# Attention with two window masks and a slot mixture on one core: constants built on chip, longer DRAM runs for phi and w1, output halves evacuated by two engines

## The chip, the cores and the metric

The kernel runs on one core of one Trainium2 chip. Its engines have instruction queues of their own and meet only at semaphores: TensorE (PE in the profile, its weight loads PEld), VectorE (DVE), ScalarE (ACT), GpSimd (POOL) and SyncE (SP). Transfers between DRAM and the on-chip memory (SBUF) are issued from an engine's queue and carried out by 16 DMA engines. Matmuls write to PSUM[...]. The metric is the time of one execution on the device in microseconds (us), median of several runs.

## The reference

Eight batches of eight-head attention over 576 positions with head dimension 64, followed by a soft mixture of experts over all 4608 rows.

```python
scores = scale * np.matmul(q, k.transpose(0, 1, 3, 2))
rel = pos[:, None] - pos[None, :]
mask_plain = (rel >= 0) & (rel < window)                                   # heads 0 to 3, window 32
mask_dil = (rel >= 0) & (rel < window * dilation) & (rel % dilation == 0)   # heads 4 to 7, dilation 4
...                                          # softmax over keys, times v, heads side by side: x, 4608 x 512
logits = x @ phi                             # 4608 x 32 slots
d = softmax(logits, over rows);  slot_input = d.T @ x          # 32 x 512
h = np.maximum(slot_input[e] @ w1[e], 0.0);  slot_out[e] = h @ w2[e]   # four slots for each of 8 experts
c = softmax(logits, over slots);  return c @ slot_out          # 4608 x 512
```

Inputs and output are fp32. q, k and v hold 9.4 MB each, w1 and w2 16.8 MB each, the output 9.4 MB.

## The kernel before

All loads are cast to fp16 on the way, and all of them but two go through one queue, POOL's. Two small constants (masks and ident) come through SP's. The order on every engine is the order of the program text: the main part stands in a manual schedule.

**Prologue.** prologue() issues the loads of batch 0 in halves (q and k of the plain heads, then of the dilated heads, line 163), the constants, v of batch 0 (lines 172 and 175), phi, and then batch 1. The constants come from DRAM as fp16 arrays made ahead of time: masks (128 x 336, additive masks with -60000 where a score is masked, and in its last 32 columns a 0/1 mask for emask), ident (the 128 x 128 identity) and orders (four 128 x 128 selection matrices, repeated in each 32-row group, that put four interleaved rows of v back in order by matmul).

**Attention, per batch b, in three slots.** slot0 holds the first score group of batch b, the dilated part of batch b-1 and the sums over rows of batch b-2; slot1 the second score group and v; slot2 the third group and the logits of batch b-1. DVE transposes raw q and k into place (qk_plain, line 241; qk_dil, line 250). emit_scores() writes the mask into two PSUM tiles of two banks each, sa and sb (line 276, ident times masks), adds q times k on top (line 287) and lets ACT take the exponent (line 298). order_v_plain() uses the same two PSUM tiles to reorder v (line 188). emit_av() multiplies by v, emit_norm() divides by the row sums into xp and xd, the normalised rows x of the plain and the dilated heads. back_logits() needs x transposed (back_xT_plain, back_xT_dil) and phi4, which is phi repeated four times; back_u() accumulates d.T @ x over the batches with x as the stationary operand (line 455), in two chunks c of 128 features for each half of the heads.

**Weights.** weights() spreads the loads of w1 over the batches (load_w1, line 220: 16 loads of two 128-row chunks of one expert) and puts w2 at the end (load_w2, line 224). The w2 of experts 6 and 7 are loaded by halves of their columns (line 232). w2 is read in 8 KB runs, since each partition takes four consecutive rows.

**Queue order on POOL.** load_qk(b+2) waits until the raw buffers (two of each) are free, load_v(b+2) until v's staging has been spread, which involves two POOL copies (lines 212 and 216) that wait for DVE (line 209). Since POOL takes its instructions in order, a copy that waits also holds the loads behind it.

**Tail.** After the attention: slot inputs, hidden layer (line 645), slot outputs by column halves (line 681). Half 0 of the columns is complete before half 1; so the first 8 of 18 row pairs store their half 0 early. combine(half, pair) computes 256 rows x 256 columns: two matmuls into PSUM (line 697), scaling by the reciprocal row sum on the way to SBUF (lines 709 and 713) and a store of 256 KB issued by POOL (line 719). combine_full(pair) does both halves, with ACT on block 0 and DVE on block 1 (lines 732 and 736), and a store of 512 KB (line 743).

Of the kernel before, what the change touches and what calls it, by code (L numbers as in the profile page):

```python
# [9 lines left out]
FP32 = mybir.dt.float32  # L10
# [9 lines left out]
WINDOW = 32  # L20
# [20 lines left out]
NE = NT + DIL + 1  # L41
NFIN = N_ROWS // 128
UNITS = 7
NH = DMODEL // 2
NSPLIT = 16


def make_masks():

    a = np.arange(128)[:, None]  # L50
    rel = np.arange(WQ)[None, :] - a
    plain = (rel >= 0) & (rel < WINDOW)
    rel = 32 + np.arange(LEFT)[None, :] - a
    left = (rel >= 0) & (rel < WINDOW) & (a < 48)
    m = [plain, plain[:, 0:TAIL]] + [left] * 5
    m = [np.where(x, 0.0, -60000.0) for x in m]
    ok = ((np.arange(128)[:, None] % 32) < LEFT) & np.ones((1, N_SLOTS), bool)
    m.append(ok)
    return np.ascontiguousarray(np.concatenate(m, axis=1).astype(np.float16))


def make_orders():

    a = np.arange(128)[:, None, None] % 32
    r = np.arange(DIL)[None, :, None]
    p = np.arange(128)[None, None, :]
    return np.ascontiguousarray((p == DIL * a + r).astype(np.float16).reshape(128, DIL * 128))


@with_exitstack  # L70
def kernel(
# [9 lines left out]
):  # L81
    nc = tc.nc

    mask_np = make_masks()
    masks_dram = nc.inline_tensor(mask_np, name="masks_d")
    orders_dram = nc.inline_tensor(make_orders(), name="orders_d")
    ident_dram = nc.inline_tensor(np.eye(128, dtype=np.float16), name="ident_d")


    consts = ctx.enter_context(tc.tile_pool(name="consts", bufs=1))  # L90
    masks = consts.tile([128, mask_np.shape[1]], FP16, name="masks")
    bias = (
        masks[:, None, 0:WQ].broadcast_to([128, 3, WQ]),
        masks[:, 0 : W1 + NLEFT],
# [73 lines left out]
    def load_v(b):  # L168
        slab = fix.tile([128, V_SLAB], FP16, name=f"vs_{b}", tag=f"vs{b % 2}")
        sa, sb = (slab[:, 2048 * i : 2048 * i + 2048].rearrange("a (h n) -> a h n", h=H) for i in range(2))  # L170
        vstage[b] = (sa, sb)
        nc.gpsimd.dma_start(
            out=sa, in_=v[b, :, 0:512, :].rearrange("h (a r) d -> a h (r d)", r=DIL)
        )
        nc.gpsimd.dma_start(
            out=sb[0:LEFT], in_=v[b, :, 512:S, :].rearrange("h (a r) d -> a h (r d)", r=DIL)
        )

    def order_v_plain(b):
# [16 lines left out]
        for ab in range(2):  # L196
# [4 lines left out]
            if ab == 0:  # L201
# [2 lines left out]
                    in_=ps[0][0:TAIL, 0, 256:512].rearrange("p (h d) -> p h d", h=4),  # L204
                )

    def spread_v(b):
        sa, sb = vstage.pop(b)
        nc.vector.tensor_copy(  # L209
            out=vD[b % NV][:, :, :, 0:D], in_=sa[:, 4:8].rearrange("a h (r d) -> a h r d", r=DIL)  # L210
        )
        nc.gpsimd.tensor_copy(
            out=vL[b % NV][32 : 32 + LEFT, :, :, 0:D],
            in_=sb[0:LEFT, 4:8].rearrange("a h (r d) -> a h r d", r=DIL),
        )
        nc.gpsimd.tensor_copy(out=vL[b % NV][0:32, :, :, 0:D], in_=vD[b % NV][96:128, :, :, 0:D])  # L216

    def load_w1(e, i):
        src = moe_w1[e].rearrange("(c p) f -> p c f", p=128)
        nc.gpsimd.dma_start(out=w1t[e][:, 2 * i : 2 * i + 2, :], in_=src[:, 2 * i : 2 * i + 2, :])  # L220

    def load_w2(e, half=None):
        if half is None:
# [13 lines left out]
    def qk_plain(ti, b):  # L237
        src = raw[(ti, b)][:, 0, :].bitcast(U32).rearrange("p (j m) -> p j m", m=32)
        t = qTp[b % 2] if ti == 0 else kTp[b % 2][:, 0:S, :]
        dst = t.rearrange("p s t -> p (s t)").bitcast(U32).rearrange("p (a j) -> p j a", j=PJ)  # L240
        nc.vector.transpose(out=dst, in_=src)  # L241
# [200 lines left out]
    def back_u(b):  # L442
        up = ring.tile([128, 5, N_SLOTS], FP32, name=f"u_{b}", tag="ring")
        er = er_t.pop(b)
        jobs = []
        for t in range(NT):
            n = 128 if t < 4 else TAIL
            for c in range(2):
                jobs.append((c, xp_t[b][0:n, t, 128 * c : 128 * c + 128], er[0:n, t, :]))
            jobs.append((4, ones[0:n, :], er[0:n, t, :]))  # L450
        for r in range(DIL + 1):
            for c in range(2):
                jobs.append((2 + c, xd_t[b][:, r, 128 * c : 128 * c + 128], er[:, NT + r, :]))
        for i, (c, l, rr) in enumerate(jobs):
            nc.tensor.matmul(  # L455
                up[:, c, :], l, rr, start=(i == 0), stop=(i == len(jobs) - 1), skip_group_check=True
            )
        if b == 0:
            nc.vector.tensor_copy(out=UT, in_=up)
        else:  # L460
            nc.vector.tensor_tensor(out=UT, in0=UT, in1=up, op=ALU.add)
# [4 lines left out]
    def prologue():  # L466
        load_qk(0, 0, (0,))
        load_qk(1, 0, (0,))
        nc.sync.dma_start(out=masks, in_=masks_dram.ap())
        nc.sync.dma_start(out=ident, in_=ident_dram.ap())  # L470
        for i in range(2):
            nc.vector.memset(kTp[i][:, S : S + 64, :], 0.0)
            nc.vector.memset(kTd[i][:, S : S + 80, :], 0.0)
            nc.vector.memset(qTd[i][:, S : S + 16, :], 0.0)
            nc.vector.memset(vP[i][:, :, :, D : D + 1], 1.0)
            nc.vector.memset(vP[i][TAIL:128, 4, :, :], 0.0)
            nc.vector.memset(vD[i][:, :, :, D : D + 1], 1.0)
            nc.vector.memset(vL[i][:, :, :, D : D + 1], 1.0)
        load_qk(0, 0, (1,))
        load_qk(1, 0, (1,))  # L480
        nc.gpsimd.dma_start(out=orders.rearrange("p r n -> p (r n)"), in_=orders_dram.ap())
        load_v(0)
        nc.gpsimd.dma_start(out=phi_raw, in_=moe_phi.rearrange("(c p) s -> p c s", p=128))
        load_qk(0, 1)
        load_qk(1, 1)
        load_v(1)
        qk_plain(0, 0)
        qk_plain(1, 0)
        nc.vector.memset(ones, 1.0)
        nc.vector.memset(emask, 1.0)  # L490
        for part in range(2):
            qk_dil(0, 0, part)
        qk_dil(1, 0, 0)
# [34 lines left out]
    def slot0(b):  # L528
        att, b1, b2, b3 = b < B, b - 1 >= 0 and b <= B, 2 <= b < B + 2, b + 1 < B
        if att:  # L530
            qk_dil(1, b, 1)
            emit_scores(b, 0)
            if b + 2 < B:
                load_qk(0, b + 2)
                load_qk(1, b + 2)
            weights(b, 0)
        if b == 0:
            nc.vector.memset(ET, 0.0)
            nc.vector.memset(siTm, 0.0)
            nc.vector.tensor_copy(out=emask[:, NE - 1, :], in_=masks[:, W1 + NLEFT :])  # L540
            nc.vector.tensor_copy(
                out=phi4, in_=phi_raw[:, :, None, :].broadcast_to([128, 4, 4, N_SLOTS])
            )
        if b1:
            emit_av(b - 1, "d", 0)
            emit_norm(b - 1, "d", 0)
        if b2:
            back_erow(b - 2)
        if b1:
            emit_av(b - 1, "d", 1)  # L550
            emit_norm(b - 1, "d", 1)
            back_xT_plain(b - 1, 0)
        if att and b > 0:
            order_v_plain(b)
        if b1:
            emit_av(b - 1, "d", 2)
            emit_norm(b - 1, "d", 2)
            back_xT_plain(b - 1, 1)
        if b2:
            back_u(b - 2)  # L560
# [132 lines left out]
    def combine(half, pair):  # L693
        fp = psum_f.tile([128, 2, NH], FP32, name=f"f{half}_{pair}", tag="f")
        r0 = 256 * pair
        for k in range(2):
            nc.tensor.matmul(  # L697
                fp[:, k, :],
                ET[:, r0 + 128 * k : r0 + 128 * k + 128],
                so_sb[:, NH * half : NH * half + NH],  # L700
                start=True,
                stop=True,
                skip_group_check=True,
            )
        ot = out_pool.tile([128, 2, NH], FP16, name=f"ot{half}_{pair}", tag=f"ot{half}", bufs=NSPLIT // 2)
        if pair % 2 == 0:
            for k in range(2):
                blk = 2 * pair + k
                nc.scalar.activation(  # L709
                    out=ot[:, k, :], in_=fp[:, k, :], func=AF.Copy, scale=rrow[:, blk : blk + 1]  # L710
                )
        else:
            nc.vector.tensor_tensor(  # L713
                out=ot,
                in0=fp,
                in1=rrow[:, 2 * pair : 2 * pair + 2, None].broadcast_to([128, 2, NH]),
                op=ALU.mult,
            )
        nc.gpsimd.dma_start(  # L719
            out=out[r0 : r0 + 256, NH * half : NH * half + NH].rearrange("(k p) n -> p k n", k=2),  # L720
            in_=ot,
        )
# [74 lines left out]
```

The softmax here doesn't subtract the row's maximum and nothing guards it: scores larger than these inputs give would overflow.

## Time and profile before

Median 184.07 us of 4 runs (183.55 to 184.17).

| | |
|---|---|
| profiled execution | 184.17 us |
| its span, first to last instruction | 182.2 us |
| busy share PE, DVE, ACT, POOL | 77%, 57%, 49%, 44% |
| DMA moved, counted as landed | 41.00 MB in 32023 packets |
| read from and written to DRAM | 62.18 MB and 9.44 MB |
| median time from issue to landing, w1 (512 KB) | 16.9 us |
| the same, v (512 KB) | 13.3 us |
| the same, orders (128 KB), masks (84 KB), ident (32 KB), phi (32 KB) | 7.1, 1.8, 2.0, 8.8 us |

The page divides the span into 40 slices of 4.56 us and gives a digit of busy tenths for each. "DMA" is the mean busy share of the 16 DMA engines and can pass 1 in the tables by window, because an engine can have more than one packet under way. A group of instructions is a line of the program, engine, operation, output <- input, shapes and count, then busy time, mean ns of one, and the idle time of the engine just before them with what ended it. A time from issue to landing contains the time that a transfer waited behind others in the queue.

### The profile page before, as it was taken

How to read it: one execution, taken by the hardware profiler on the slowest of the kernel's cores; microseconds unless marked ns; L12 is line 12 of the kernel's file. 1: busy time of each engine (PE TensorE's matmuls, PEld its weight loads, DVE VectorE, ACT ScalarE, POOL GpSimd, SP SyncE). 2: the span in 40 equal slices, each digit the busy share in tenths (PEclk: the TensorE clock that was granted, in tenths of full speed). 3: DMA queues.
4: the chain of work that ended last, by engine and by line, in shares of the span. 5: the costliest groups of instructions: out<-in, count | busy, mean ns of one | idle time of the engine just before them, and what ended most of it. 6: DMA issues, size and time to landing. Idle time of an engine off the chain costs nothing.

```text
span 182.2 us, 5521 instructions
## 1 busy us (share of the span) xinstructions
PE 141.1 (77%) x2448; PEld 84.9 (47%) x2448; DVE 104.1 (57%) x225; ACT 89.8 (49%) x161; POOL 80.8 (44%) x112
## 2 busy tenths in 40 slices
PE   3157989999999999999999999998695076786000
PEld 0034556567557557557557557573532063332000
DVE  2686787858767867867867865360502002599000
ACT  2053357667666766766766766734002004698000
POOL 7643644652651751751823836311101111996820
PEclk9999999999999999999999999995559657899655
DMA  5999999999999999999999999999999999999995
GB/s 88 193 200 214 199 208 204 214 208 204 212 208 205 212 210 204 213 209 203 212 210 203 211 211 213 216 216 213 216 212 215 199 196 158 329 397 409 408 409 138
DMA packets 32023, 41.00 MB, mean 225 GB/s; under 512 B 2144, under 2 KB 19680, under 8 KB 32000
## 3 DMA queue, kind: packets, MB, share of 16 engines
q0 software_dynamic: 31712, 40.54, 119.5%
q8 instruction: 19, 0.31, 0.6%
q1 hardware_dynamic: 288, 0.12, 0.2%
q14 instruction: 4, 0.03, 0.0%
HBM read 62.18 MB, written 9.44 MB: 393 GB/s over the span
## 4 chain that ended last, share of the span: by engine, by line
DMA 48%; PE 21%; issue 10%; POOL 9%; DVE 3%; ACT 3%; POOLq 1%
DMA w<-in_moe_w_dram 42%; DMA raw<-in_q_dram 6%; PE o_p L344 4%; PE lg L413 4%; PE sa L287 3%; PE sa L276 3%; ACT p L298 3%; PE sb L276 2%; POOL out_dram L719 2%; POOL out_dram L743 2%; POOL raw L163 1%; DVE of L736 1%; PE rd L394 1%; PE u L455 1%; PE vb L188 1%
## 5 line engine op out<-in xcount | busy, mean ns | idle before, releaser
L298 ACT ACTIVATE p<-sa 128x960 f16<-128x960 f32 (+2 forms) x24 | 21.4, 891 | 30.0 <-PE sb L287 29.2
L344 PEld LDWEIGHTS <-p 128*128 128x128 f16 (+2 forms) x544 | 19.5, 98 | 12.6 <-issue 8.6
L241 DVE STREAM_TRANSPOSE qk<-raw 128x576 uint32<-128x576 uint32 x16 | 20.0, 1250 | 6.4 <-DMA raw<-in_q_dram 5.2
L250 DVE STREAM_TRANSPOSE qk<-raw 128x320 uint32<-128x320 uint32 (+1 forms) x32 | 21.6, 677 | 0.3
L298 ACT ACTIVATE p<-sb 128x960 f16<-128x960 f32 (+2 forms) x24 | 21.2, 884 | 0.0
L216 POOL COPY v<-v 32x1024 f16<-32x1024 f16 x8 | 8.3, 1036 | 25.0 <-DVE v L209 24.9
L287 PE MATMUL sa<-qk 32*128 32x160 f16 (+4 forms) x416 | 15.7, 212 | 3.8 <-DVE qk L241 3.8
L413 PE MATMUL lg<-xTd,phi 128*128 128x288 f16 x32 | 18.3, 659 | 0.0
L232 POOL DMA_DIRECT2D w<-in_moe_w_dram x8 | 5.9, 743 | 27.6 <-DMA w<-in_moe_w_dram 23.2
L287 PEld LDWEIGHTS <-qk 32*128 32x128 f16 x832 | 11.9, 96 | 13.3 <-issue 8.2
L276 PE MATMUL sa<-masks,ident 128*128 128x480 f16 (+2 forms) x48 | 13.9, 374 | 4.9 <-DMA ident<-ident_d 3.2
L344 PE MATMUL o_p<-v,p 128*128 128x65 f16 (+1 forms) x288 | 16.3, 201 | 0.7 <-ACT v L197 0.7
L276 PEld LDWEIGHTS <-ident 128*128 128x128 f16 x96 | 9.0, 103 | 15.8 <-issue 8.9
L287 PE MATMUL sb<-qk 32*128 32x160 f16 (+4 forms) x416 | 15.7, 212 | 0.0
L366 DVE TENSOR_TENSOR xd<-o_d,rc_d 128x448 f16<-128x448 f32 (+1 forms) x24 | 14.4, 602 | 0.8
L366 DVE TENSOR_TENSOR xp<-o_p,rc_p 128x448 f16<-128x448 f32 (+1 forms) x24 | 14.4, 602 | 0.8
L276 PE MATMUL sb<-masks,ident 128*128 128x480 f16 (+2 forms) x48 | 14.0, 372 | 0.5 <-issue 0.3
L713 DVE TENSOR_TENSOR ot<-f,rrow 128x512 f16<-128x512 f32 x8 | 5.5, 688 | 15.4 <-PE f L697 15.4
L719 POOL DMA_DIRECT2D out_dram<-ot x16 | 11.3, 712 | 6.7 <-ACT ot L709 6.7
L220 POOL DMA_DIRECT2D w<-in_moe_w_dram x16 | 11.3, 710 | 5.8 <-DMA w<-in_moe_w_dram 2.1
L681 PE MATMUL so<-w,hTm 128*32 128x256 f16 x128 | 6.8, 346 | 9.0 <-DMA w<-in_moe_w_dram 8.2
L188 PE MATMUL va<-vs,orders 32*128 32x256 f16 (+1 forms) x96 | 12.1, 289 | 1.0 <-ACT p L298 1.0
(86 smaller groups left out, 264.6 us busy)
## 6 DMA issues: line engine op xcount, KB each, us to landing
w<-in_moe_w_dram POOLq DMA_DIRECT2D x16, 512.0 KB, 16.9
w<-in_moe_w_dram POOLq DMA_DIRECT2D x6, 1024.0 KB, 27.9
out_dram<-of POOLq DMA_DIRECT2D x10, 512.0 KB, 6.3
vs<-in_v_dram POOLq DMA_DIRECT2D x8, 512.0 KB, 13.3
out_dram<-ot POOLq DMA_DIRECT2D x16, 256.0 KB, 4.7
raw<-in_q_dram POOLq DMA_DIRECT2D x7, 576.0 KB, 15.3
raw<-in_k_dram POOLq DMA_DIRECT2D x7, 576.0 KB, 15.6
w<-in_moe_w_dram POOLq DMA_DIRECT2D x8, 256.0 KB, 24.0
```

Of the source, the lines that this page charges most:

```text
L188: nc.tensor.matmul(o.rearrange("p (h d) -> p h d", h=4), l, st[:, 0:4, D * r : D * r + D], start=(r == 0), stop=(r == DIL - 1), skip_group ...
L216: nc.gpsimd.tensor_copy(out=vL[b % NV][0:32, :, :, 0:D], in_=vD[b % NV][96:128, :, :, 0:D])
L220: nc.gpsimd.dma_start(out=w1t[e][:, 2 * i : 2 * i + 2, :], in_=src[:, 2 * i : 2 * i + 2, :])
L241: nc.vector.transpose(out=dst, in_=src)
L250: nc.vector.transpose(out=o, in_=i)
L276: nc.tensor.matmul(sps[h // 2][:, h % 2, 0:n], ident, bias[g], start=True, stop=False, skip_group_check=True,)
L287: nc.tensor.matmul(sps[h // 2][:, h % 2, c0 : c0 + w], kt_[32 * h : 32 * h + 32, k0 : k0 + 128, tt], qt_[32 * h : 32 * h + 32, q0 : q0 + w ...
L298: nc.scalar.activation(out=pt, in_=sps[ab][:, :, 0:n], func=AF.Exp, scale=SCALE)
L344: nc.tensor.matmul(o[p0 : p0 + np_, n, :], l, rr, start=(k == 0), stop=(k == len(jobs) - 1), skip_group_check=True,)
L366: nc.vector.tensor_tensor(out=x.rearrange("p t (h d) -> p (t h) d", h=4)[0:nq, u0:u1, :], in0=o[0:nq, 0:n, 0:D], in1=rc[0:nq, 0:n, None].b ...
L413: nc.tensor.matmul(lp, phi4[:, kc].rearrange("p c s -> p (c s)"), rhs, start=(kc == 0), stop=(kc == 3))
L719: nc.gpsimd.dma_start(out=out[r0 : r0 + 256, NH * half : NH * half + NH].rearrange("(k p) n -> p k n", k=2), in_=ot,)
```

## The change

1. **Constants built on chip.** masks, ident and orders are no longer loaded. DVE fills masks with 0 and ones and the first 32 rows of orders with 1 at the start of the prologue. POOL then cuts them by affine_select, which keeps an element where an affine expression of partition and column passes a comparison, and else writes a fill value: five of them after the four half loads of q and k and before load_v(0), a sixth (orders, 32 x 512) after load_v(0). DVE copies the 64 columns of masks that repeat, before its first transpose, and copies orders to the other three 32-row groups after it has set emask. The last row block of emask is a row sum over orders instead of a mask column.
2. **phi.** It is loaded with four consecutive rows on each partition, 512 B in a run where there were four of 128 B, and later in the queue, behind batch 1. A new function order_phi() puts the rows in order with 16 matmuls against orders in the PSUM tiles sa and sb, and ACT copies the result to phi4. It is called in slot0 of batch 1, after order_v_plain. The DVE copy that made phi4 goes.
3. **w1.** Each partition takes two consecutive rows of w1, so a run in DRAM has 8 KB instead of 4 KB, and the row order changes. back_u() follows it by taking the features of x with a step of two as its stationary operand.
4. **Output halves.** combine() no longer alternates between ACT (two pieces of 128 x 256) and DVE (one of 128 x 512) from pair to pair: ACT does block 0 and DVE block 1 of every pair.

```diff
     def load_w1(e, i):
-        src = moe_w1[e].rearrange("(c p) f -> p c f", p=128)
-        nc.gpsimd.dma_start(out=w1t[e][:, 2 * i : 2 * i + 2, :], in_=src[:, 2 * i : 2 * i + 2, :])
+        nc.gpsimd.dma_start(
+            out=w1t[e][:, 2 * i : 2 * i + 2, :].rearrange("p l f -> p (l f)"),
+            in_=moe_w1[e, 256 * i : 256 * i + 256].rearrange("(p l) f -> p (l f)", l=2),
+        )
...
+    def order_phi():
+        ps = [psum_s.tile([128, 2, 512], FP32, name=f"phi{ab}", tag=f"s{ab}") for ab in "ab"]
+        for r in range(DIL):
+            for c in range(4):
+                nc.tensor.matmul(
+                    ps[c // 2][:, c % 2, 0:128].rearrange("p (u s) -> p u s", u=4),
+                    orders[32 * c : 32 * c + 32, r, :],
+                    phi_raw[32 * c : 32 * c + 32, r, None, :].broadcast_to([32, 4, N_SLOTS]),
...
+        for ab in range(2):
+            nc.scalar.copy(
+                out=phi4[:, 2 * ab : 2 * ab + 2].rearrange("p c u s -> p c (u s)"),
+                in_=ps[ab][:, :, 0:128],
+            )
...
         for t in range(NT):
...
             for c in range(2):
-                jobs.append((c, xp_t[b][0:n, t, 128 * c : 128 * c + 128], er[0:n, t, :]))
+                x = xp_t[b][0:n, t, :].rearrange("p (x l) -> p l x", l=2)
+                jobs.append((c, x[:, c, :], er[0:n, t, :]))
...
     def prologue():
         load_qk(0, 0, (0,))
         load_qk(1, 0, (0,))
-        nc.sync.dma_start(out=masks, in_=masks_dram.ap())
-        nc.sync.dma_start(out=ident, in_=ident_dram.ap())
+        nc.vector.memset(masks, 0.0)
+        nc.vector.memset(ones, 1.0)
+        nc.vector.memset(orders[0:32], 1.0)
...
         load_qk(0, 0, (1,))
         load_qk(1, 0, (1,))
-        nc.gpsimd.dma_start(out=orders.rearrange("p r n -> p (r n)"), in_=orders_dram.ap())
+        left = masks[:, W1:].rearrange("p (u c) -> p u c", c=LEFT)
+        band = (
+            (ident, ones, [[1, 128]], 0, -1, ALU.is_equal, 0.0),
+            (masks[:, 0:WQ], masks[:, 0:WQ], [[1, WQ]], 0, -1, ALU.is_ge, MASKED),
+            (masks[:, 0:WQ], masks[:, 0:WQ], [[-1, WQ]], WINDOW - 1, 1, ALU.is_ge, MASKED),
+            (left, left, [[0, 5], [1, LEFT]], 32, -1, ALU.is_ge, MASKED),
+            (left, left, [[0, 5], [-1, LEFT]], -1, 1, ALU.is_ge, MASKED),
+        )
+        for dst, src, pattern, base, mult, op, fill in band:
+            nc.gpsimd.affine_select(
...
         load_v(0)
-        nc.gpsimd.dma_start(out=phi_raw, in_=moe_phi.rearrange("(c p) s -> p c s", p=128))
+        nc.gpsimd.affine_select(
+            out=orders[0:32],
...
         load_qk(0, 1)
         load_qk(1, 1)
         load_v(1)
+        nc.gpsimd.dma_start(out=phi_raw, in_=moe_phi.rearrange("(p l) s -> p l s", l=4))
+        nc.vector.tensor_copy(out=masks[:, WQ:W1], in_=masks[:, 0:TAIL])
         qk_plain(0, 0)
         qk_plain(1, 0)
-        nc.vector.memset(ones, 1.0)
         nc.vector.memset(emask, 1.0)
+        for i in range(1, 4):
+            nc.vector.tensor_copy(out=orders[32 * i : 32 * i + 32], in_=orders[0:32])
...
-            nc.vector.tensor_copy(out=emask[:, NE - 1, :], in_=masks[:, W1 + NLEFT :])
+            nc.vector.tensor_reduce(
+                out=halves, in_=orders[:, 0, 0:TAIL], axis=mybir.AxisListType.X, op=ALU.add
+            )
             nc.vector.tensor_copy(
-                out=phi4, in_=phi_raw[:, :, None, :].broadcast_to([128, 4, 4, N_SLOTS])
+                out=emask[:, NE - 1, :], in_=halves.broadcast_to([128, N_SLOTS])
             )
...
         if att and b > 0:
             order_v_plain(b)
+        if b == 1:
+            order_phi()
...
-        if pair % 2 == 0:
...
+        blk = 2 * pair
+        nc.scalar.activation(
+            out=ot[:, 0, :], in_=fp[:, 0, :], func=AF.Copy, scale=rrow[:, blk : blk + 1]
+        )
+        nc.vector.tensor_scalar(
+            out=ot[:, 1, :],
+            in0=fp[:, 1, :],
+            scalar1=rrow[:, blk + 1 : blk + 2],
...
```

## The prediction

> **What bounds the kernel now.** I read the page's slices and its chain first, to see which resource is never idle, then the table by stages for the rates of each kind of transfer, then the order of POOL's work at the start and the waits at the end.
>
> ```profile
> DMA  5999999999999999999999999999999999999995
> GB/s 88 193 200 214 199 208 204 214 208 204 212 208 205 212 210 204 213 209 203 212 210 203 211 211 213 216 216 213 216 212 215 199 196 158 329 397 409 408 409 138
> ```
> ```profile
> DMA 48%; PE 21%; issue 10%; POOL 9%; DVE 3%; ACT 3%; POOLq 1%
> ```
>
> The DMA engines are full from the second slice to the last but one. Until about 155 us they load (bytes are counted as they land, half as many as were read, since the loads cast fp32 to fp16), after that they store. PE is at 9 tenths for 105 us too, so two candidates stand; the landing times decide between them. A v load of 512 KB lands 13.3 us after its issue:
>
> ```profile
> vs<-in_v_dram POOLq DMA_DIRECT2D x8, 512.0 KB, 13.3
> w<-in_moe_w_dram POOLq DMA_DIRECT2D x16, 512.0 KB, 16.9
> ```
>
> Its own bytes need 2.7 us at 196 GB/s, and an empty queue delivers some 1.3 us after the issue (first issue at 1.27 us, first loads moving at 2.6). The other 9 us are queue. So what POOL waits for (24.9 us for DVE's copy of v, 12.1 us for the transposes) only shortens a queue that stays about 9 us deep: compute may slip by that much before a transfer starts later. The stages, in the view by windows (us, busy times by engine, clock, DMA share, GB/s):
>
> ```profile
> 2.60:9.00 6.40, 2.03 (x14) 0.69 (x18) 2.80 (x4) 0.00 (x0) 5.12 (x8) 1.00 1.04 178
> 12.30:13.50 1.20, 0.75 (x49) 0.64 (x48) 1.20 (x1) 0.39 (x1) 0.00 (x0) 1.00 1.74 192
> 101.50:111.40 9.90, 9.68 (x167) 5.95 (x164) 6.80 (x17) 6.74 (x10) 6.00 (x8) 1.00 1.12 210
> 119.00:140.00 21.00, 17.95 (x275) 10.41 (x272) 6.57 (x21) 5.32 (x13) 2.97 (x4) 0.67 1.06 214
> 153.00:155.00 2.00, 2.00 (x10) 1.17 (x8) 1.38 (x2) 1.91 (x5) 0.79 (x2) 0.50 0.83 112
> 156.50:160.50 4.00, 2.94 (x19) 1.20 (x19) 2.60 (x4) 3.05 (x8) 3.96 (x6) 1.00 1.86 373
> 163.00:178.50 15.50, 3.91 (x18) 1.63 (x17) 5.22 (x8) 4.62 (x10) 9.50 (x14) 0.72 1.62 409
> ```
>
> Third row: w1 alone (4 KB runs in DRAM) at 210. Fourth: w2 alone (8 KB runs, the form that w1 gets) at 214. Fifth: the one hole, where the last weights drain and no store has been issued yet. Sixth: eight stores of 256 KB, each 0.71 us of POOL issue, which is 368 GB/s: POOL sets the rate here. Seventh: DMA sets it again.
>
> **What the Trainium skill says.** "DMA: Bandwidth & Descriptors", section "Why small descriptors are slow (HBM only)": every packet carries a fixed overhead, so fewer and longer ones move the same bytes sooner. The trace agrees in direction: v's 1 KB runs move at 196 GB/s, w1's at 210, w2's at 214. "GPSIMD Engine Reference", section "Performance pitfalls for Q7 kernels": a compare-and-select body costs 1.03 to 2.03 cycles an element; section "Performance versus the Vector engine" converts cycles at 1.2 GHz, so 0.9 to 1.7 ns. No affine_select is in this trace; POOL's copies run at 1036 ns for 1024 elements, 1.0 ns each, inside that band. "TensorE: Matmul & The Clock Gate", "Weight-path perf modes": the fast weight load also takes strided columns. The trace has weight loads with a stride of four at 113 ns beside 91 ns for contiguous ones.
>
> **The change part by part**, against the profiled execution (184.17 us, span 182.2).
>
> *w1 as 8 KB runs.* 16 loads of 512 KB are 8.39 MB as landed: 8.39/210 = 39.95 us now, 8.39/214 = 39.20 us then. Minus 0.75 us on the queue that is never empty. Bounds: 0 if the rate is not the run's doing, 0.9 at 215. I take 0.75. The features of x are interleaved in back_u instead, so 20 of its 25 weight loads a batch (ten of xp, ten of xd) get a stride of two: at most 22 ns each from the pair above, 0.44 us of PE per batch, 3.5 us over eight. It is hidden by the queue's depth.
>
> *Constants.* The load of orders (128 KB, not cast, so a byte landed is a byte read: the stream reads 2 x 204 GB/s, 131/408 = 0.32 us) leaves the queue: minus 0.3, bounds 0.2 to 0.6. masks and ident (116 KB on SP) move before 2.6 us, while the first q load is still on its way: 0 to 0.2, I take 0.05. phi goes from 512 packets to 128: the second row holds it, 230 KB of which 33 KB are phi; the other 197 KB at 205 need 0.96 us, leaving 0.24 us for phi, against 0.16 by bytes alone. Minus 0.05, bounds -0.1 to 0.1.
>
> *What POOL does instead.* The order of its first issues:
>
> ```profile
> 1.27 0.68 POOL L163 DMA_DIRECT2D raw<-in_q_dram  x1 [0.82 <-POOLq L781]
> ...
> 3.01 0.56 POOL L163 DMA_DIRECT2D raw<-in_k_dram  x1
> 3.54 0.58 POOL L481 DMA_DIRECT2D orders<-orders_d  x1
> 4.07 0.94 POOL L172 DMA_DIRECT2D vs<-in_v_dram  x1
> 4.96 0.59 POOL L175 DMA_DIRECT2D vs<-in_v_dram  x1
> 5.49 0.82 POOL L483 DMA_DIRECT2D phi_raw<-in_moe_phi_dram  x1
> 6.25 0.76 POOL L158 DMA_DIRECT2D raw<-in_q_dram  x1
> ```
>
> Five selects now stand between 3.54 us and load_v(0): 128 + 160 + 160 + 80 + 80 = 608 elements, at 1.0 to 1.7 ns 0.6 to 1.0 us, plus some 0.1 us each (POOL's one-element memsets take 0.09): 1.1 to 1.5 us. v is issued at about 5.0 instead of 4.07. The four half loads before it are 1.18 MB; at 178 GB/s from 2.6 us they last to 9.2. v must be issued 1.3 us ahead, by 7.9: the selects have 4.35 us of cover. The sixth select (512 elements, 0.6 to 1.0 us) follows the two v issues, at about 6.5; q(1) is issued near 7.4 instead of 6.25 and is needed only when v has moved, at about 12. Cost: nothing. DVE's copy inside masks waits for the selects until 5.0 and stands ahead of the first transpose, which begins at 5.93 anyway; mask matmuls start near 5.2 rather than 3.17, take 1.8 us, and qk matmuls come at 8.74. DVE gets three memsets (0.2 to 0.5 us each) and three copies of orders (0.36 each, by the phi broadcast that goes) before qk_dil: about 1 us late, PE's second score group with it.
>
> *phi reordered on PE.* In batch 1, 16 small matmuls at 0.05 us (the pace of v's), after ACT has emptied the two banks, then two ACT copies of 128x256 (0.37 each, as so_sb's), and only then the scores' masks, which use the same banks: 0.8 + 0.74 + latency, PE late by about 1.7 us, once; DVE's copy of v and POOL's second v copy behind it too, and the loads POOL issues next. Together with the prologue (1) and back_u (six batches before the last v issue, 2.6) that is 5.3 us at worst against 9 us of queue. After the attention the same delay, 6.2 us at most, meets PE's waits for w2 (8.2 us in all).
>
> *Output halves by two engines.* Now:
>
> ```profile
> L709 ACT ACTIVATE ot<-f,rrow 128x256 f16<-128x256 f32 x16 | 6.6, 470 | 1.3 <-PE f L697 1.2
> L713 DVE TENSOR_TENSOR ot<-f,rrow 128x512 f16<-128x512 f32 x8 | 5.5, 688 | 15.4 <-PE f L697 15.4
> POOL out_dram L719 <- ACT ot L709: 6.7, 1, 6.7
> ```
>
> The two first lines are groups, the third a wait. Pair 0 is two ACT pieces in a row, so the first store waits for the second. Afterwards DVE makes it beside ACT; 0.40 us by half of L736's 746 ns plus overhead. The first store leaves about 0.3 us sooner, into the hole of 153 to 155. But weights still drain there until after 156, and a DMA engine with weights left gains nothing: 0 to 0.3, I take 0.1. The other pairs move nothing: 0.47 us a pair on either engine is under POOL's 0.71.
>
> Sum: 0.75 + 0.3 + 0.05 + 0.05 + 0.1 = 1.25 us. Span 182.2 - 1.25 = 180.95; 1.97 lie outside it: 182.9. The profiled run is 0.1 above the median, so **182.8** against 184.07. A measurement tells about 0.3% (0.55 us) from no change.
>
> **Rivals.**
> *POOL runs the queue dry (slower).* Each select beyond 4.35 us in sum is a hole. The GPSIMD page, "Instruction dispatch", prices the first call of a freshly loaded routine at about 6 us: then the selects take 7.4, a hole of 3.1, less the gain of 1.25: 186.0. It decides from selects of 5.6 us (1.1 us each). Against it: POOL's first copy here, 1.03 us, is no longer than its later ones.
> *Compute uses up the queue (slower).* If strided loads or order_phi cost twice my worst, 10.6 us against 9 less the 0.75 that DMA gained: 2.4 us later, 185.3. For it: PE is at 9 tenths; against: 22 ns is for twice the stride.
> *Row length does nothing (same).* w1 stays at 210, its slightly lower rate being the attention's doing: only 0.5 us remain, 183.6.
> *More than summed.* If the slow start (147 GB/s between 2.6 and 5.5 us) was due to the constants, up to 0.9 more: 181.9.
>
> **How the numbers follow.** Likeliest case 66% (182.2 to 183.5 by its bounds), no effect 13%, POOL 9%, compute 6%, more 6%. Faster 72%, same 13%, slower 15%. The range 182.0 to 184.6 holds the first two cases and leaves out the slower ones.
>
> **What would show it.** w1 stretches at 214 GB/s and its landings shorter; no slice under 190 GB/s at the start; selects of 0.2 to 0.4 us and v issued before 7.9; POOL still waiting for compute while v lands over 8 us after issue; the first store 1.4 us sooner. A low second slice, or v landing within 5 us of its issue, would prove me wrong.

## The result, and the profile after

The changed kernel takes 184.39 us (median of 43 runs, 183.44 to 186.69) where the kernel before, run beside it, takes 183.78 (64 runs). The ratio is 1.0026, 95% interval 1.0015 to 1.0038: slower by a quarter of a per cent, where 182.8 and a faster kernel were forecast. That 184.39 lies within the stated range of 182.0 to 184.6 is luck: the range was drawn round a gain and round no effect, and a loss by what happens at the end was no case of it. Two of the later profiles, of after_spstore and after_split6, are of an execution 1.2 and 1.6% longer than the median of their kernels; of these two only lengths and rates are read.

The transfers did roughly what the forecast said. The page's slices (40 of 4.57 us), and the landing times:

```profile
DMA  4999999999999999999999999999999999999994
GB/s 63 195 164 215 198 211 207 210 211 207 208 210 208 210 211 210 207 212 207 210 209 208 214 214 212 215 213 214 214 215 215 197 196 167 371 359 406 408 410 94
```
```profile
vs<-in_v_dram POOLq DMA_DIRECT2D x8, 512.0 KB, 10.2
w<-in_moe_w_dram POOLq DMA_DIRECT2D x16, 512.0 KB, 14.1
```

The last slice moves 94 GB/s, not 138: the stores end sooner. The third moves 164 instead of 200. The stages in the view by windows (length; busy time of PE, PEld, DVE, ACT and POOL; clock; DMA share; GB/s), with the stretch of the third slice added:

```profile
9.00:12.00 3.00, 1.77 (x22) 0.55 (x16) 2.89 (x6) 1.83 (x2) 2.26 (x4) 1.00 1.18 140
...
101.50:111.40 9.90, 9.90 (x201) 6.12 (x201) 8.35 (x17) 6.76 (x12) 5.94 (x8) 1.00 1.07 214
119.00:140.00 21.00, 18.62 (x257) 10.13 (x257) 7.23 (x22) 5.95 (x13) 2.96 (x4) 0.76 1.07 215
153.00:155.00 2.00, 2.00 (x17) 0.81 (x15) 2.00 (x6) 1.84 (x5) 1.45 (x3) 0.50 0.84 122
...
163.00:178.50 15.50, 3.86 (x20) 1.69 (x18) 6.29 (x12) 5.34 (x11) 10.01 (x14) 0.74 1.62 408
```

w1 alone moves at 214 instead of 210, as forecast. From 9 to 12 us only 140 GB/s move; before it was 204:

```profile
9.00:12.00 3.00, 1.75 (x28) 0.88 (x20) 2.70 (x5) 1.83 (x2) 2.13 (x3) 1.00 1.31 204
```

In the trace the last packet (a packet is the piece that a DMA engine moves at a time) of a store starts at 179.46 us (before 180.37), 0.9 us sooner. And yet the span is 182.7 us instead of 182.2. What lies between is in the view of the instructions that close the program (ns min/median/max, then first and last start in us). Before:

```profile
L792 POOLq DRAIN  x3: 51/91/7855, 173.6 to 182.0; - x3
L792 SPq DRAIN  x3: 7/7/7, 181.2 to 181.7; - x3
```

And after:

```profile
L819 POOLq DRAIN  x3: 51/86/9044, 172.9 to 182.4; - x3
L819 SPq DRAIN  x3: 7/7/7, 180.2 to 182.2; - x3
```

SP waits for the last stores and reaches its first DRAIN when they have landed: 181.2 before, 180.2 after, 1.0 us sooner. POOL's first DRAIN stands behind its last store issue; it lasts 7.86 us from 173.63, to 181.49, and after the change 9.04 us from 172.88, to 181.93. All engines meet behind it: the span ends 0.75 us after it before and 0.73 after the change. (The Trainium skill, "VectorE: DVE Perf Modes", "The DRAIN you can't avoid", has the DRAINs at a program's ends at a constant 12 ns or so on all five engines; SP's are 7 ns in these traces, but POOL's first takes the 7.86 and 9.04 us.) So POOL closed 0.28 us after SP reached its first DRAIN before, and 1.71 us after it with the change. Below this distance is called the **excess**.

The sum from profile to profile: stores seen to land -0.99, excess +1.43, steps behind the drain -0.02, outside of the span 1.70 instead of 1.93 (spans of 182.66 and 182.24), -0.23; together +0.19, as between the profiled times of 184.17 and 184.36. The questions are what the drain does, which part of the change makes it longer, and what the hole of 9 to 12 us cost.

### The profile page after: what moved, and what is told of

Same layout as the page of the kernel before. It is cut to its first block, busy times and chain, and to the rows that moved or that the text cites. A ratio compares the mean times of both kernels' runs of the same rounds, so it can differ in the third digit from the quotient of the medians.

```text
span 182.7 us, 5579 instructions
## 1 busy us (share of the span) xinstructions
PE 143.7 (79%) x2464; PEld 85.6 (47%) x2464; DVE 108.2 (59%) x239; ACT 91.5 (50%) x163; POOL 80.4 (44%) x117
## 3 DMA queue, kind: packets, MB, share of 16 engines
HBM read 61.93 MB, written 9.44 MB: 391 GB/s over the span
## 4 chain that ended last, share of the span: by engine, by line
PE 44%; DMA 30%; POOL 7%; ACT 6%; issue 5%; DVE 3%; POOLq 1%
DMA w<-in_moe_w_dram 22%; PE lg L407 8%; PE o_p L338 7%; ACT p L292 6%; PE sa L281 6%; DMA raw<-in_q_dram 5%; PE sa L270 5%; PE sb L270 4%; DMA out_dram<-of 3%; PE u L451 3%; PE rd L388 2%; PE vb L162 2%; PE va L162 2%; PE rp L376 2%; PE f L757 1%
## 5 line engine op out<-in xcount | busy, mean ns | idle before, releaser
L270 PE MATMUL sa<-masks,ident 128*128 128x480 f16 (+2 forms) x48 | 14.6, 389 | 6.2 <-POOL masks L487 4.8
L281 PE MATMUL sa<-qk 32*128 32x160 f16 (+4 forms) x416 | 16.2, 215 | 2.0 <-DVE qk L235 1.9
L338 PE MATMUL o_p<-v,p 128*128 128x65 f16 (+1 forms) x288 | 16.8, 203 | 0.7 <-ACT v L171 0.7
L270 PEld LDWEIGHTS <-ident 128*128 128x128 f16 x96 | 9.2, 106 | 16.8 <-issue 7.4
L281 PE MATMUL sb<-qk 32*128 32x160 f16 (+4 forms) x416 | 16.3, 215 | 0.0
L226 POOL DMA_DIRECT2D w<-in_moe_w_dram x8 | 5.9, 744 | 23.3 <-DMA w<-in_moe_w_dram 20.8
L739 DVE TENSOR_SCALAR ot<-f,rrow 128x256 f16<-128x256 f32 x16 | 7.3, 482 | 11.2 <-ACT ot L736 11.2
L411 ACT ACTIVATE ET<-lg 128x288 f16<-128x288 f32 x16 | 6.6, 411 | 11.7 <-PE lg L407 11.5
L381 ACT COPY xTp<-rp 128x576 f16<-128x576 f16 x16 | 10.4, 647 | 1.8 <-PE rp L376 1.8
## 6 DMA issues: line engine op xcount, KB each, us to landing
vs<-in_v_dram POOLq DMA_DIRECT2D x8, 512.0 KB, 10.2
```

What stands on the lines that cost most here:

```text
L270: nc.tensor.matmul(sps[h // 2][:, h % 2, 0:n], ident, bias[g], start=True, stop=False, skip_group_check=True,)
L281: nc.tensor.matmul(sps[h // 2][:, h % 2, c0 : c0 + w], kt_[32 * h : 32 * h + 32, k0 : k0 + 128, tt], qt_[32 * h : 32 * h + 32, q0 : q0 + w ...
L338: nc.tensor.matmul(o[p0 : p0 + np_, n, :], l, rr, start=(k == 0), stop=(k == len(jobs) - 1), skip_group_check=True,)
L381: nc.scalar.copy(out=xTp_t[b][:, c, :], in_=rg)
```

## The experiments

**Each part alone.** w1_only is the kernel before with the new load_w1 and the new pieces of x in back_u:

```diff
-        nc.gpsimd.dma_start(out=w1t[e][:, 2 * i : 2 * i + 2, :], in_=src[:, 2 * i : 2 * i + 2, :])
+        nc.gpsimd.dma_start(out=w1t[e][:, 2 * i : 2 * i + 2, :].rearrange("p l f -> p (l f)"),
+            in_=moe_w1[e, 256 * i : 256 * i + 256].rearrange("(p l) f -> p (l f)", l=2))
```

evac_only is the kernel before with the new combine(); const_only is the changed kernel with load_w1, back_u, combine() and phi as before. No kernel has phi's part alone.

> The kernel before with 8 KB runs of w1 and the stride of two in back_u, nothing else. Theory of the prediction (each part acts by itself on a DMA queue that never runs dry): 0.75 us faster than before, w1 stretches at 214 GB/s instead of 210. Rival (row length does nothing to the end, the gain is lost behind it): within 0.3 us of before.

> The kernel before with output halves made by ACT and DVE together, nothing else. Theory: first store issued 0.3 us earlier, end 0 to 0.3 us earlier. Rival (the end of the kernel is set by something after the last store's data, POOL's closing drain): time changes by up to 1 us in either direction although the stores' data end no later.

> The kernel before with masks, ident and orders built on chip, phi as before. Theory of a hole at the start (after: 140 GB/s between 9 and 12 us, before: 204): the hole is here too, at least 0.15 MB are missing between 9 and 12 us, and it costs more than the 0.3 us that the load of orders gave back: 0.5 us slower than before. Rival (the hole comes from phi or from chance): 204 GB/s there and 0.3 us faster.

| | median us | ratio to before, 95% | last packet | shifted (see below) | excess |
|---|---|---|---|---|---|
| before | 183.78 | | 180.37 | 179.98 | 0.28 |
| changed | 184.39 | 1.0026 (1.0015 to 1.0038) | 179.46 | 179.49 | 1.71 |
| w1_only | 184.71 | 1.0042 (1.0027 to 1.0058) | 179.41 | 179.58 | 1.75 |
| evac_only | 184.04 | 1.0008 (0.9990 to 1.0027) | 180.08 | 180.35 | 0.36 |
| const_only | 183.76 | 0.9983 (0.9969 to 0.9997) | 179.62 | 180.05 | 0.34 |

The three add up to +0.33%, the whole change was +0.26%. The loss is w1's, 0.8 us where a gain of 0.75 or no change was expected: its stores end sooner, as they should, and its drain closes 1.75 us after SP. const_only has the hole too (148 GB/s from 9 to 12 us), yet it is 0.17% faster and not 0.5 us slower. The closing instructions of w1_only, view as above:

```profile
L796 POOLq DRAIN  x3: 51/91/9322, 172.7 to 182.5; - x3
L796 SPq DRAIN  x3: 7/7/7, 180.2 to 182.3; - x3
```

One profile's last packet is good to 0.4 to 0.8 us only: in before_lastwait and after_lastwait below, which are the same programs up to there, it came at 179.99 instead of 180.37 and at 180.30 instead of 179.46. Much of this is the execution: a profiled one can be 0.9 us shorter than the median of its kernel or 1.1 us longer. The column "shifted" takes that difference off. It is an estimate from these numbers, and it puts before_lastwait at 180.03 and after_lastwait at 179.69. By it w1 moved the last packet forward by 0.4 us and the whole change by 0.3 to 0.5, not by 0.9.

**The drain by itself.** Four one-element memsets on POOL, each on the source tile of one of the last four stores, make POOL wait for these stores before it closes:

```diff
+        for t in last_ot[-4:]:
+            nc.gpsimd.memset(t[:, 0, 0:1], 0.0)
```

> The changed kernel, and at its end four one-element memsets on POOL that wait until the last four stores have landed, so that POOL reaches its closing drain only then. Theory of the tail (in the profile of the changed kernel the stores' data end 0.9 us earlier than before, and POOL's closing drain ends 0.4 us later): the drain is short and the time falls by 1.0 to 1.5 us. Rival (the drain waits for something that takes as long from the last landing): no change, within 0.3 us of the changed kernel.

> The kernel before, and at its end four one-element memsets on POOL that wait for the last four stores, so that POOL's closing drain begins only when they have landed. With the changed kernel this drain then took 4.04 us, so the end came later. Theory A (the drain is a fixed piece of work): 4.0 us here too, time 3 to 3.7 us above before. Theory B (the drain works off what the descriptor rings have accumulated, and 4 KB packets of w1 leave more of it): clearly under 4 us here, 2 to 3 us or less, time at most 2 us above before.

```profile
L825 POOLq DRAIN  x3: 51/86/4044, 180.8 to 185.3; - x3
```
```profile
L798 POOLq DRAIN  x3: 51/91/1431, 180.5 to 182.4; - x3
```

With the stores landed the changed kernel's drain still takes 4.04 us and the earlier one's 1.43. Neither of the outcomes expected of after_lastwait, a gain or no change, came. So the drain is more than waiting for stores: it has work of its own, 2.6 us more after the change. Without the memsets part of the work runs while stores land; with them all of it lies behind: 186.98 us (+2.6) for the changed kernel, 184.56 (+0.7) for the one before.

after_spstore lets SP issue the stores, from fp32 tiles, so that they need no cast, and with fewer of these tiles:

```diff
-        nc.gpsimd.dma_start(out=out[r0 : r0 + 256 ...
+        nc.sync.dma_start(out=out[r0 : r0 + 256 ...
-        ot = out_pool.tile([128, 2, NH], FP16, ... bufs=NSPLIT // 2)
+        ot = out_pool.tile([128, 2, NH], FP32, ... bufs=(8, 4)[half])
-        ot = out_pool.tile([128, 2, DMODEL], FP16, ... bufs=8)
+        ot = out_pool.tile([128, 2, DMODEL], FP32, ... bufs=3)
```

> The changed kernel with its stores taken from POOL's queue to SP's, the output tiles in fp32[...] and fewer of them. POOL's last transfer is then the last load of w2, its closing drain begins near 147 us and is over long before the end. Theory of the tail (the drain after the last store, 1.7 us, hides the gain of w1): the end follows the last landing by under 1.3 us, and the time falls to 182.5 to 183.3. Rival (the drain isn't the cause; the end is set by the stores): within 0.4 us of the changed kernel.

```profile
L819 POOLq DRAIN  x3: 51/98/11379, 148.7 to 184.9; - x3
```
```profile
163.00:178.50 15.50, 6.77 (x25) 2.54 (x23) 8.27 (x15) 7.36 (x14) 0.00 (x0) 0.87 1.03 369
```

POOL's drain is over at 160.1, out of the way, but the stores move at 369 GB/s instead of 408: 184.65 us, ratio 1.0043 (1.0016 to 1.0069), where 182.5 to 183.3 was expected. By the two rates the 9.44 MB of stores take 2.4 us longer (an estimate), more than the 1.7 us that the drain could give back. Whether SP's queue, the fp32 tiles or their smaller number makes the stores slower was not separated.

**Half of w1, and all but w1.** w1_half is the kernel before with 8 KB runs for the first load of each expert only (i = 0, with the strided pieces of xp in back_u). after_no_w1 is the changed kernel with load_w1 and back_u as before. The lines that w1_half adds to w1_only's load_w1:

```diff
     def load_w1(e, i):
+        if i == 1:
+            src = moe_w1[e].rearrange("(c p) f -> p c f", p=128)
+            nc.gpsimd.dma_start(out=w1t[e][:, 2 * i : 2 * i + 2, :], in_=src[:, 2 * i : 2 * i + 2, :])
+            return
```

> The kernel before with 8 KB runs for the first 256 features of each expert's w1 alone, 4 KB for the rest: half of the packets saved. The stream gains 0.4 to 0.5 us by its rate. Theory B (the drain grows with what the longer packets leave): drain between 7.86 and 9.32 us, near 8.6, the time 0.2 to 0.5 us above before. Theory R (where the rings stand at the end decides, not how much was saved): any drain from 7.8 to 12 us, not between. If the drain is at 7.5 to 7.9, ending with the last landing, the time is 0.4 us below before.

> The changed kernel with w1 in 4 KB runs and back_u as before: everything but the third part. If the parts add up (constants -0.15, halves +0.1, measured alone) it is within 0.3 us of before, and 0.4 to 0.8 us faster than the changed kernel; its closing drain ends within 0.5 us of SP's seeing the last store landed. If phi or the sum of the parts costs time, it is as slow as the changed kernel.

w1_half: 183.36 us, ratio 0.9978 (0.9963 to 0.9992), excess 0.20, so half of w1's change gains 0.48 us and costs nothing at the end. after_no_w1: 183.70, 0.9987 (0.9968 to 1.0005), excess 0.41:

```profile
L815 POOLq DRAIN  x3: 51/86/7790, 172.5 to 180.8; - x3
L815 SPq DRAIN  x3: 7/7/7, 179.9 to 180.6; - x3
```

By then I held a **packet theory**. The queue of POOL carries 1982 packets per DMA engine before and 1827 after; the drain alone took 1.43 and 4.04 us; so it would grow by 16.8 ns for each packet by which the queue falls short of some 2067.

**The packet theory tested.** after_split6 gives the packets back by the stores: six of the ten full-width stores as two of half the columns. before_split8 does it to eight of them in the kernel before. w1_half_lastwait is w1_half with the four memsets.

```diff
+        if 11 <= pair <= 16:      # before_split8: 10 to 17
+            for h in range(2):
+                nc.gpsimd.dma_start(
+                    out=out[r0 : r0 + 256, NH * h : NH * h + NH].rearrange("(k p) n -> p k n", k=2),
+                    in_=ot[:, :, NH * h : NH * h + NH])
+            return
```

> The changed kernel; six of its ten full-width output stores (pairs 11 to 16, 2 KB runs) are issued as two stores of half the columns each (1 KB runs), so the queue has 1536 packets more: 30768, 1923 per DMA engine against 1827. Nothing else differs. Packet theory (POOL's closing drain grows as the queue's packets per DMA engine fall short of about 2050): 125 short, about as w1_half (130 short, drain ended 0.20 us after SP saw the last store), so the drain's excess falls from 1.71 to 0.2 to 0.5 us and the time by 1.2 to 1.5 us, to 182.9 to 183.3, although POOL issues six stores more (4.2 us at 0.71). Rival, the loads themselves (8 KB runs of w1 cost time in POOL's drain whatever the count): excess stays near 1.7 and the time at 184.4 or above. Third: POOL's six further issues make it the bound of the last stage, then the last packet comes 1 us or more after 179.5.

> The kernel before; all eight full-width stores of the last eight pairs issued as two halves each: 2048 packets more, 33760, 2110 per DMA engine against 1982. It asks what lies beyond the count at which the fit gives zero (about 2067). If the drain fills up a ring of a fixed length of some 2048 packets, 2110 lie in a second round and the drain would have far more to do: (2 x 2048 - 2110) x 16.8 ns = 33 us, a time near 210. If it falls to nothing and stays there, the excess is 0 to 0.35 us and the time 183.5 to 184.2. If the count has nothing to do with it, the same.

> w1_half (w1 with 8 KB runs in half of its loads, 1918 packets per DMA engine) with four one-element memsets on POOL after the last store, each waiting for one of the last four stores, so that POOL's closing drain begins when the stores have landed and its own length shows. Packet theory: the fit through 1.43 us at 1982 and 4.04 us at 1827 gives 1.43 + 64 x 16.8 ns = 2.5 us. Rival, a step rather than a slope (w1_half's drain was hidden as well as that of before): about 1.4 us as in before.

Two of the three went against it. after_split6 took 185.09 us (1.0071, 1.0039 to 1.0103) and its excess was 2.09 instead of 0.2 to 0.5. before_split8, at 2118 packets, decides little: an excess of 0.61 is neither a drain of tens of us nor the 0 to 0.35 of the other outcome (184.54 us; its stores moved at 380 GB/s in the stage of 409, POOL being busy with issues for 14.39 of 15.5 us). And at 1918 packets the drain alone was no longer than at 1982, where the theory asked for 2.5 us:

```profile
L805 POOLq DRAIN  x3: 51/91/1267, 179.9 to 181.6; - x3
```

So the drain has two lengths here, and not a slope.

**What else makes it long.** Two kernels lower the packets with w1 as before: the w2 of both experts 6 and 7, or of 6 alone, loaded whole (8 KB runs) instead of by column halves (1 KB runs). Two raise them with w1 as changed: more store packets (the split of six) or more load packets (expert 5's w2 by halves too). All four have the memsets.

```diff
# before_w2whole_lastwait (before_w2one_lastwait: 6 alone)
-            for half in range(2):
-                for e in HALVED:
-                    load_w2(e, half)
+            for e in HALVED:
+                load_w2(e)
# after_three_lastwait
-    HALVED = (6, 7)
-    ORDER = (0, 1, 4, 2, 3, 5) + HALVED
+    HALVED = (5, 6, 7)
+    ORDER = (0, 1, 4, 2, 3) + HALVED
...
-            load_w2(5)
```

> The kernel before with its last two w2 experts loaded whole (two loads of 8 KB runs) instead of by column halves (eight loads of 1 KB runs), and the four memsets that let POOL's closing drain show its own length. w1 stays at 4 KB runs; the queue has 3584 packets fewer, 1758 per DMA engine, fewer than the changed kernel's 1827. If the drain's length follows the number of packets (of loads: 1316 against 1540 before, 1385 changed), it takes 4 us or more. If it is the form of w1's loads, it takes 1.3 to 1.5 us as in before. The time itself may differ by the weights' arrival and isn't read.

> The same with one of the two experts whole: 1870 packets per DMA engine (loads 1428), between w1_half (1918, drain 1.27 us alone) and w1_only (1854, excess 1.75). By packets: about 4 us if there is a step above 1870, 1.3 if it lies below. By the form of w1: 1.3 to 1.5 us.

> The changed kernel with six full-width stores issued as halves (1929 packets per DMA engine, all w1 in 8 KB runs) and the four memsets. By the number of all packets, 1929 is above w1_half's 1918, so the drain alone takes 1.3 us. By the loads' packets alone (1385) or by w1's form it takes about 4.0 us, as without the split.

> The changed kernel (all of w1 in 8 KB runs) with a third w2 expert (5) loaded by column halves (1 KB runs) instead of whole, and the four memsets. That gives the loads 112 packets per DMA engine more: 1942 in all, about 1500 of them loads. If it is the number of the loads' packets that makes the drain long, it is short again, 1.0 to 1.5 us alone, although all of w1 has 8 KB runs. If it is w1's runs or anything else about the changed kernel, it stays at 4.0 to 4.5. The time isn't read: more 1 KB runs make the loads slower.

The closing drains, in this order:

```profile
L797 POOLq DRAIN  x3: 51/91/4209, 185.5 to 190.2; - x3
```
```profile
L799 POOLq DRAIN  x3: 51/91/861, 183.1 to 184.5; - x3
```
```profile
L832 POOLq DRAIN  x3: 51/86/4536, 180.3 to 185.3; - x3
```
```profile
L824 POOLq DRAIN  x3: 51/86/4289, 180.1 to 184.9; - x3
```

| drain alone | packets per DMA engine | of them loads | us |
|---|---|---|---|
| before | 1982 | 1540 | 1.43 |
| w1_half | 1918 | 1476 | 1.27 |
| before, one w2 whole | 1867 | 1425 | 0.86 |
| before, two w2 whole | 1752 | 1310 | 4.21 |
| changed | 1827 | 1385 | 4.04 |
| changed, six stores split | 1929 | 1385 | 4.54 |
| changed, third w2 by halves | 1942 | 1500 | 4.29 |

Each length is that of one profiled execution. The drain is long without w1's new form (4.21), so that form is not needed for it. It is long at 1942 packets and short at 1867, so the number of packets alone does not decide; with loads at 1500 it is long and at 1425 short, so the number of the loads' packets alone doesn't either. A joint rule, of the form and the number together, is not excluded, nor is one by where in the sequence of its queue the kernel stops.

By the Trainium skill, "DMA: Bandwidth & Descriptors", "SWDGE vs HWDGE vs iDMA", POOL writes the descriptors of its transfers into rings from which the DMA engines read; no run here shows how they are freed. That the drain clears what has built up there is a guess. Rules of this kind can be fitted afterwards to the issue and landing times of the traces. But two of them with numbers as different as 335 packets per DMA engine issued since the last clearing and 554 not yet cleared both sort the kernels of the table, so a fit says little, and no run was made to try one. The cause of the two lengths stays open.

**The hole at the start, and the best version.** after_v_first issues v(0) ahead of the selects. after_v_half adds w1_half's loads to it, no_w1_v_first adds w1 as before.

```diff
+        load_v(0)
         for dst, src, pattern, base, mult, op, fill in band:
             nc.gpsimd.affine_select(
...
-        load_v(0)
```

> The changed kernel with the two issues of v(0) ahead of the five selects, so v is issued at about 3.8 us instead of 5.23. It asks what made the hole of 9 to 12 us (140 GB/s against 204 before). If v's descriptors came too late, the hole goes: 185 GB/s or more there. If DVE's copies of orders beside POOL, or POOL's selects, slow the transfer itself, it stays below 165. For the end: about 0.2 MB are missing in the hole, 1 us of queue; where loads are what sets the end, closing it moves the last weight packet and the last store forward by up to 1 us, and the time to 183.4; where the hole is made up for by later slack, the time stays within 0.3 us of 184.4.

> The changed kernel with v(0) issued ahead of the selects and 8 KB runs only for the first half of each w1 expert (1891 packets per DMA engine, loads 1449). If its drain is short as in w1_half (excess 0.2 to 0.4 us), the last packet at about 179.1 gives 182.6 to 183.0, the best so far. If the drain is long (excess 1.7), 184.0 to 184.4.

> The changed kernel with w1's loads as before (4 KB runs), which had a short closing drain (excess 0.41), and with v(0) issued ahead of the selects, which moved the last store packet 0.77 us forward. If the two add: last packet at about 178.4, excess 0.4, 183.70 - 0.5 to 0.77 = 182.9 to 183.2, the best version here. If the drain turns long again (excess 1.7 or more, as in after_v_half), 184.3 or more.

POOL's timeline (start, us, instruction), first of the changed kernel, then of after_v_first, and the same window of 9 to 12 us as above for the latter:

```profile
3.75 0.29 POOL L487 TENSOR_SCALAR_AFFINE_SELECT ident<-ones 128x128 f16<-128x128 f16 x1
4.00 1.29 POOL L487 TENSOR_SCALAR_AFFINE_SELECT masks<-masks 128x160 f16<-128x160 f16 x4
5.23 0.94 POOL L146 DMA_DIRECT2D vs<-in_v_dram  x1
...
6.73 0.66 POOL L497 TENSOR_SCALAR_AFFINE_SELECT orders<-orders 32x512 f16<-32x512 f16 x1
```
```profile
3.59 0.93 POOL L146 DMA_DIRECT2D vs<-in_v_dram  x1
4.47 0.60 POOL L149 DMA_DIRECT2D vs<-in_v_dram  x1
5.19 0.29 POOL L488 TENSOR_SCALAR_AFFINE_SELECT ident<-ones 128x128 f16<-128x128 f16 x1
```
```profile
9.00:12.00 3.00, 1.77 (x24) 0.72 (x16) 2.91 (x6) 1.83 (x2) 1.97 (x4) 1.00 1.34 180
```

With v issued 1.64 us sooner 180 GB/s move in the hole, and the last packet comes at 178.69 instead of 179.46 (shifted as above, 179.04 instead of 179.49). The time is 183.89 (1.0002, 0.9986 to 1.0018), 0.24% less than the changed kernel, with the same excess of 1.71. DVE's copies of orders come 0.25 us later but still within the hole (from 8.95 us), so v's late issue was most of it. The other profiles agree: 140 to 161 GB/s in the eight kernels with v behind the selects, 180 to 184 in the three with v ahead, 198 or more where orders was loaded.

after_v_half, 184.23 us (1.0024, 1.0006 to 1.0041), has an excess of 1.92: there the half of w1 that cost nothing in w1_half makes the drain long. no_w1_v_first has a short one:

```profile
L815 POOLq DRAIN  x3: 51/86/7760, 172.7 to 180.9; - x3
L815 SPq DRAIN  x3: 7/7/7, 180.1 to 180.7; - x3
```

It takes **182.87 us** beside 183.72 of before: 0.9946 (0.9927 to 0.9964), faster than both kernels. Against after_no_w1 (0.9987) v's place is worth 0.41%, 0.75 us. Its last packet came at 179.34, not at the 178.4 expected, and that of after_no_w1 at 179.18; but the profiled execution of after_no_w1 is 0.9 us shorter than its median, and shifted as above the packet moves from 180.12 to 179.32.

## Why the prediction was wrong

**The step that failed: "Span 182.2 - 1.25 = 180.95; 1.97 lie outside it".** It carried everything from the last landing to the end over as a constant. In the two profiles the DMA ended 0.91 us sooner and POOL's drain 0.44 us later, because the drain, which had ended 0.28 us past SP's sight of the last store, ended 1.71 past it. That the drain is what lost it is shown by its length with the stores out of the way (1.43 and 4.04 us), by w1_only, with the DMA gain and the later end, and by w1_half and after_no_w1, where the excess is 0.20 and 0.41 and no loss is measured. Why the drain has two lengths is not known. The DRAIN of 7.86 us was in the trace of before; that it ended after SP's and had work of its own could have been asked, and no rival did.

**w1, -0.75: right in direction on the DMA, about half in size, wrong as time.** The rate went from 210 to 214 in the two profiles, as said. But the same stretch ran at 210 to 213 in all nine profiles with w1's loads as before (mean 211.2) and at 212 to 214 in the eight with all of them changed (mean 213.5). By these means the 8.39 MB gain 0.4 us (an estimate), and so does the last packet, shifted. As a part alone w1 is +0.42%, +0.8 us. The strided weight loads, priced at 22 ns each at most, cost almost nothing: 98 ns (xp) and 97 (xd) in the median against 96 and 96.

**The selects, "Cost: nothing": wrong.** Their durations were right (0.29 us, 0.32 each for the masks, 0.66 for orders against 0.6 to 1.0), so was v's issue (5.23 against about 5.0) inside the limit of 7.9. The limit was wrong: it took the 1.3 us from issue to first packet of an empty queue's first q load, and asked only that v begin in time. v did: its first packets start at 8.72 us, 3.5 after the issue, and the half loads' last at 9.44. With v first they start no sooner, at 8.75. But from 9.5 to 12 us 301 of v's packets start per us, and with v first 363. So v began in time and flowed too slowly; what holds it back is not shown. By the view by windows (GB/s times length, summed from 1 to 30 us) 5.29 MB had landed, with v first 5.43: 0.14 MB, 0.7 us at 205 GB/s, beside the 0.45 and 0.75 us of the two timed pairs. Before it was 5.56, 0.25 of it the constants that the change no longer loads, so by 30 us the hole had taken back what they gave. The rival of a dry queue had the place and the sign, but not the mechanism: the 6 us that the Trainium skill, "GPSIMD Engine Reference", "Instruction dispatch", gives for a freshly loaded routine did not occur (the first select took 0.29). The estimate of 0.9 to 1.7 ns an element from that page's "Performance pitfalls for Q7 kernels" agrees for orders: 659 ns for 512, 1.3 each.

**Constants, phi and halves, -0.5 together.** The kernel after_no_w1, which has them, measures 0.13% less, which is not clear of noise. With v ahead of the selects it is 0.54%, 1.0 us (0.7 to 1.3), more than the term; but there v also goes out 0.49 us sooner than in the kernel before. Which part gives more is not resolved. The halves alone lie between 0.10% faster and 0.27% slower. The first store left at 153.56 instead of 154.21, 0.65 us sooner where 1.4 was forecast; with the halves alone it left at 154.39, no sooner at all, and in the changed kernel weights went on landing until 156.2. phi's sixteen matmuls took 0.44 us where 0.8 was forecast, its two copies 0.37 and 0.38, as said, and they hid: v still lands 10.2 us after its issue.

**The rivals.** "Row length does nothing" fell with the rates of w1, if by about half of what was forecast. "Compute uses up the queue" fell: from the fourth slice to the 33rd no slice is under 196 GB/s. "More than summed" may be right of the constants (above), not of the start: 152 GB/s between 2.6 and 5 us against 144.

## What to carry to other kernels

The last landing is not the end: see which engine's closing drain ends last and by how much, and ask what it waits for, before a gain on the DMA is counted as time. A longer run or fewer packets on POOL's queue can change that drain by more than they save, so measure the end with each half of such a change. Issue a load ahead of compute on the issuing engine, and don't take its lead time from the first load of the program: 3.5 us from v's issue to its first packet were too short a lead here, and 5.2 us brought most of the rate back.

## What the runs showed of the hardware

POOL's closing drain has two lengths here, 0.9 to 1.4 us and 4.0 to 4.5, behind stores that have landed. affine_select takes 0.29 us for 128 columns and 0.66 for 512 (fp16, 128 and 32 partitions). Stores from fp32 tiles through SP's queue, with three full-width tiles instead of eight, moved at 369 GB/s where POOL's, cast from fp16, moved at 408. Weight loads with a stride of two columns cost 1 to 2 ns more than contiguous ones (97 and 98 ns against 96). Loads of w1 cast to fp16 landed at 210 to 213 GB/s in 4 KB runs and at 212 to 214 in 8 KB runs.
